# Attention scores in three fp32r products of split q and k, in row halves of TensorE, two units at a time

## The chip, the core and the metric

The kernel runs on one core of one Trainium2 chip. The metric is the time of one execution in device microseconds (us); each value is the median of several runs. One execution was recorded by the hardware profiler, and its page and its trace are what is read below. TensorE is written PE, its weight loads PEld, VectorE DVE, ScalarE ACT, GpSimd POOL, and SyncE, which issues most transfers, SP.

## The reference

An attention with a sigmoid in place of the softmax feeds a mixture of experts that sends each token to one of eight experts:

```python
B, H, S, D = 8, 12, 448, 64
scores = q @ k.transpose(0, 1, 3, 2) / sqrt(D) - log(S)      # per batch and head, 448 x 448
attn = 1 / (1 + exp(-scores))
x = (attn @ v)                                                # to 3584 tokens x 768

logits = x @ w_gate                      # 3584 x 8
e_idx = argmax(logits, axis=1)
gate_w = softmax(logits)[n, e_idx]
for e in range(8):
    h = maximum(x[mask_e] @ w1[e], 0)    # 768 -> 1024
    out[mask_e] = gate_w * sigmoid(x @ w_output_gate)[mask_e, e] * (h @ w2[e])
```

All inputs and the output are fp32. The choice of the expert hangs on the largest of eight logits, so the attention is computed to fp32 accuracy.

## The kernel before

Two heads that share the 128 rows of a tile form a pair (head 0 in rows 0 to 63, head 1 in rows 64 to 127); there are 48 pairs. Two pairs form a group, and the 24 groups run one after the other, each in 7 units (`U = 7`): units 0 to 2 take 128 keys each of the first pair, units 4 to 6 those of the second, and unit 3 the last 64 keys of both pairs. Unit `u` is unit `i` of group `g` (`divmod(u, U)`), 168 units in all.

The loop of `attention` (L698 to L718) goes through the units. In each step it calls `scores(u)` and then `values(u - 2)` (`LAG = 2`). Below, S stands for the scores of one unit and V for the values of one unit.

- `scores` (L619) issues four matmuls of 64 rows by 64 columns of weights, one in each quarter of PE's array (the list `corners`): row half `j` is the head, column half `h` one half of the keys. The operands are fp32, 448 columns stream, and the trace records each such matmul as two instructions, each with its own weight load. The results lie in two banks of PSUM, one for each head; `self.ps_s` has two such pairs of banks, taken in turn. ACT then applies the sigmoid to 128x896 numbers and writes the buffer `at[u % 3]` (L627).
- `values` (L629) issues four matmuls in the same quarters, with 64x64 weights of v and the sigmoids as streaming operand. They add up in four banks (`self.ps_o`). When a pair is complete, DVE copies one bank to `xh` (L637 or L641), adds the other (L647) and transposes into the row buffer (L648).
- After three groups a batch is complete, and `gates` (L671) multiplies its result with the router's weights: 24 matmuls of 64x32 weights and 224 columns, 48 instructions in the trace (L679), at unit 3 of the next group. DVE then forms the routing lists with small operations, and POOL scatters them.
- SP loads q and k two groups ahead (L609, L610) and v (L615, L617), each in three buffers. The loads of a group are issued at unit 0 (q, k) and unit 1 (v).

During the last 50 units (`unit`, L723) the first expert slot is prepared by all engines beside the attention. Then come the expert slots, where PE works on fp32r products of 128x128 weights: each operand is split into a rounded high part and the remainder, and three of the four products are taken (L458 to L460 and L485 to L487).

`carve` gives names to parts of two large buffers, `rounded` (fp32r) and `plain` (fp32), which the expert slots use later. The order on each engine is the order in which the code issues; waits between engines are set by the data.

Of the kernel before, what the change touches and what calls it, by code (L numbers as in the profile page):

```python
# [8 lines left out]
F32 = mybir.dt.float32  # L9
# [3 lines left out]
AF = mybir.ActivationFunctionType  # L13
ALU = mybir.AluOpType
# [5 lines left out]
B, H, S, D = 8, 12, 448, 64  # L20
# [9 lines left out]
G = 2  # L30
# [3 lines left out]
W = 6  # L34
# [7 lines left out]
LATE_N = LATE_MAX + 1  # L42
KT = 8
LG = 3
OOB = 1 << 20
LROWS = E * CAP // 128
ROUNDED = (12 * DF + 12 * TB) * 4
# [4 lines left out]
def r32(ap):  # L52
    return ap.bitcast(F32)


class Kernel:
# [52 lines left out]
    def lists(self, n, g, i):  # L109
        o = i * LG * GB_ * W  # L110
        return self.hb[0:32, o:o + n * g * W].bitcast(I32).rearrange("p (a b w) -> p a b w", b=g, w=W)
# [70 lines left out]
    def init_list(self):  # L182
# [3 lines left out]
        for w in range(1, 4):  # L186
            nc.gpsimd.memset(li[:, :, w:w + 1], w)
        nc.gpsimd.memset(li[:, :, 4:5], OOB)
        nc.gpsimd.dma_start(self.lst.rearrange("(p r) w -> p r w", p=128), li)
# [392 lines left out]
    def attention(self, pool):  # L582
        nc = self.nc
        N = B * NPAIR
        NG = N // G
        GB = NPAIR // G
        U = 7
        t = lambda n, shape: pool.tile(shape, F32, name=n)
        qr = [t(f"q{i}", [128, G, S]) for i in range(3)]
        kr = [t(f"k{i}", [128, G, S]) for i in range(3)]  # L590
        vv = [t(f"v{i}", [128, G, 4, 2, D]) for i in range(3)]
        at = [t(f"a{i}", [128, 2, S]) for i in range(3)]
# [9 lines left out]
        half = [slice(0, 64), slice(64, 128)]  # L602
        corners = [(0, 0), (1, 0), (0, 1), (1, 1)]

        def load_qk(g):
            b, hp = divmod(G * g, NPAIR)
            for r in ([slice(0, G)] if g else [slice(i, i + 1) for i in range(G)]):
                src = lambda a: a[b, hp + r.start:hp + r.stop].rearrange("g p s -> p g s")
                nc.sync.dma_start(kr[g % 3][:, r], src(self.kT))  # L609
                nc.sync.dma_start(qr[g % 3][:, r], src(self.qT))  # L610

        def load_v(g):
            b, hp = divmod(G * g, NPAIR)
            v = vv[g % 3]
            nc.sync.dma_start(v[:, :, 0:3], self.vm[b, hp:hp + G].rearrange("g p c j d -> p g c j d"))  # L615
            for i in range(G):
                nc.sync.dma_start(v[half[i], i, 3], self.ve[b, hp + i])  # L617

        def scores(u):  # L619
            g, i = divmod(u, U)  # L620
            q, k = qr[g % 3], kr[g % 3]
            ps = self.take("s", self.ps_s)
            for j, h in corners:
                e, o = (h, 384) if i == 3 else (i // 4, 128 * (i % 4) + 64 * h)
                qk = nc.tensor.matmul(ps[half[h], j, 0:S], k[half[j], e, o:o + 64], q[half[j], e], start=True, stop=True)  # L625
            self.beat[1] = qk.ins
            self.beat[0] = nc.scalar.activation(at[u % 3], ps[:, :, 0:S], AF.Sigmoid, bias=self.bias_s, scale=1.0 / math.sqrt(D)).ins  # L627

        def values(u):  # L629
            g, i = divmod(u, U)  # L630
            v, a = vv[g % 3], at[u % 3]
            for h, j in corners:
                e, c = (h, 3) if i == 3 else (i // 4, i % 4)
                nc.tensor.matmul(self.ps_o[e][h][half[j], 0:S], v[half[h], e, c, j], a[half[h], j],  # L634
                                 start=(i in ((0, 3 if h else 4)[e],)), stop=(i == (2 + (h == 0), 6)[e]))
            if i == 2:
                nc.vector.tensor_copy(xh, self.ps_o[0][1][:, 0:S])  # L637
            elif i == 3:
                evict(G * g)
            elif i == 6:  # L640
                nc.vector.tensor_copy(xh, self.ps_o[1][1][:, 0:S])  # L641
                evict(G * g + 1)

        def evict(m):
            b, hp = divmod(m, NPAIR)
            x, o = xts[m % NPAIR], xt[b % 2]
            nc.vector.tensor_tensor(x, xh, self.ps_o[m % 2][0][:, 0:S], ALU.add)  # L647
            nc.vector.transpose(o[:, :, 32 * hp:32 * hp + 32], x.rearrange("p (u t) -> p u t", t=32))  # L648
            if hp == NPAIR - 1:
                dst = self.x_dram[b * S:(b + 1) * S].rearrange("(u t) (i x) -> i t u x", t=32, i=4)  # L650
                for i in range(4):
                    e = nc.scalar if m == N - 1 and i % 2 else nc.sync
                    e.dma_start(dst[i], o[32 * i:32 * i + 32])
# [3 lines left out]
        def routing(at, u):  # L657
            if routes and want[0] == at:
                want[0] = next(routes[0])
                if want[0] == "rows":  # L660
                    first = u + 2 if len(rows) != B - 3 else U * NG - 18
                    rows.append((first, routes.pop(0)))
                    if routes:
                        want[0] = next(routes[0])

        def scatters(u):
            for first, r in rows:
                if u - first in (0, 2, 3, 5):
                    next(r)

        def gates(b):  # L671
            gp, gl = self.ps_o[1], self.R["num"].rearrange("p c x -> p (c x)")
            for m in range(NPAIR // 2):
                for p in range(2):
                    e = NPAIR // 2 * p + m
                    for i in range(2):
                        c, tk = slice(64 * p + 32 * i, 64 * p + 32 * i + 32), slice(HS * i, HS * i + HS)
                        for h in range(2):
                            nc.tensor.matmul(gp[h][c, 0:HS], wg[half[h], e], xts[e][half[h], tk], start=(m == 0),  # L679
                                             stop=(m == NPAIR // 2 - 1), tile_position=(64 * h, 64 * p + 32 * i))  # L680
            nc.vector.tensor_copy(gl, gp[1][half[0], 0:HS])
            for h, p in ((1, 1), (0, 0), (0, 1)):
                nc.vector.tensor_tensor(gl, gl, gp[h][half[p], 0:HS], ALU.add)
            routes.append(self.route(b))
            if len(routes) == 1:
                want[0] = next(routes[0])
# [10 lines left out]
        LAG = 2  # L697
        for u in range(U * NG + LAG):  # L698
            g, i = divmod(u, U)
            if i == 0 and 0 < g < NG - 2:  # L700
                load_qk(g + 2)
            self.unit(u - U * NG)
            for r, name in ((2, "counts"), (3, "places")):
                if i == r:
                    routing(name, u)
            if u < U * NG:
                scores(u)
            if u >= LAG:
                values(u - LAG)
            if i == 3 and g and g % GB == 0:  # L710
                gates(g // GB - 1)
            if i == 1 and 0 < g < NG - 2:
                load_v(g + 2)
            if i == 6:
                routing("logits", u)
            scatters(u)
            if u == 10:
                self.init_list()  # L718
# [42 lines left out]
    def build(self, phases="abc"):  # L761
# [17 lines left out]
        def lists():  # L779
            i = 0  # L780
            for tab, lt, lx, n, o in ((self.tab_l, self.lts, self.lxs, LATE_N, EARLY), (self.tab_b, self.ltb, self.lxb, E, 0)):
                for a in range(0, n, LG):
                    b = min(a + LG, n)
                    lq = self.lists(b - a, lx.shape[2], i % 2)
# [86 lines left out]
```

## Time and profile before

| | before |
|---|---|
| median of 3 runs | 770.58 us (769.16 to 772.1) |
| profiled execution | 769.2 us, of which the span from first to last instruction is 767.2 us |
| granted clock of PE | 0.999 of full speed |
| PE busy | 756.8 us (99%) |
| PEld busy | 582.1 us (76%) |
| DVE busy | 398.7 us (52%) |
| ACT busy | 373.4 us (49%) |
| POOL busy | 269.2 us (35%) |

The busy time of an engine is the time in which at least one of its instructions runs. The attention takes the first 269 us of the span, the experts the rest. Matmuls overlap, so a matmul's own duration says less than the distance from its start to the start of the next; the views in order of time give starts. Weight loads run beside matmuls, so their share is no share of the time.

### The profile page before, as it was taken

What the parts mean: (1) busy time and instruction counts of PE and PEld (TensorE: products, weight loads), DVE (VectorE), ACT (ScalarE), POOL (GpSimd) and SP (SyncE); (2) the same over time, 40 slices, a digit from 0 to 9 for tenths busy, and PEclk for the clock granted to TensorE, in tenths of its full rate; (3) what the DMA queues carried; (4) which work ended last, traced back from release to release, by engine and by line L of the source; (5) the groups of instructions that cost most, each with busy time, mean ns of one, the idle gap of its engine ahead of it and who ended that gap; (6) DMA issues with size and microseconds to landing.
All of it is one profiled execution on the core that took longest, in us unless ns stands there. A gap on an engine that the chain in (4) does not pass through costs nothing. (4 is left out here: it accounts for less than half of the span.)

```text
span 767.2 us, 14868 instructions
## 1 busy us (share of the span) xinstructions
PE 756.8 (99%) x5819; PEld 582.1 (76%) x5819; DVE 398.7 (52%) x731; ACT 373.4 (49%) x429; POOL 269.2 (35%) x379
## 2 busy tenths in 40 slices
PE   9999999999999999999999999999999999999996
PEld 4444444444444489999999999999999999999996
DVE  1364746556687769523714525525615524445564
ACT  5666666666787733422523523424424424334544
POOL 5002112020444346258336137127127217316261
PEclk9999999999999999999999999999999999999999
DMA  8475766756796545447446346335345354364531
GB/s 291 132 200 135 204 146 169 205 134 169 262 306 189 156 109 201 141 102 228 125 144 217 113 139 215 120 131 190 110 167 161 130 163 132 130 211 165 176 135 41
DMA packets 73560, 126.53 MB, mean 165 GB/s; under 512 B 15410, under 2 KB 53324, under 8 KB 73472
## 3 DMA queue, kind: packets, MB, share of 16 engines
q1 hardware_dynamic: 62768, 100.18, 43.2%
q0 software_dynamic: 9776, 24.53, 9.5%
q8 instruction: 50, 0.82, 0.5%
q10 hardware_dynamic: 928, 0.69, 0.4%
q14 instruction: 38, 0.31, 0.1%
HBM read 108.77 MB, written 23.09 MB: 172 GB/s over the span
## 5 line engine op out<-in xcount | busy, mean ns | idle before, releaser
L627 ACT ACTIVATE a<-ps,bias_s 128x896 f32<-128x896 f32 x168 | 169.0, 1007 | 86.0 <-PE ps L625 85.4
L384 POOL DMA_INDIRECT plain<-x_dram,lxs x112 | 138.0, 1232 | 73.2 <-ACT h L470 24.7
L625 PE MATMUL ps<-q,k 64*64 64x448 f32 x1344 | 158.1, 542 | 0.0
L634 PE MATMUL ps<-a,v 64*64 64x448 f32 x1344 | 156.2, 536 | 0.2 <-DMA v<-vm 0.2
L458 PE MATMUL ps<-rounded 128*128 128x448 f32 (+1 forms) x432 | 150.7, 349 | 1.2 <-ACTq L822 1.2
L459 PE MATMUL ps<-rounded 128*128 128x448 f32 (+1 forms) x432 | 149.9, 347 | 0.0
L460 PE MATMUL ps<-rounded 128*128 128x448 f32 (+1 forms) x432 | 149.9, 347 | 0.0
L485 PE MATMUL ps<-w2h,h 128*128 128x384 f32 x400 | 133.7, 334 | 0.8 <-DVE y L532 0.8
L487 PE MATMUL ps<-w2h,h 128*128 128x384 f32 x400 | 133.7, 334 | 0.0
L486 PE MATMUL ps<-w2l,h 128*128 128x384 f32 x400 | 133.6, 334 | 0.0
L410 DVE TENSOR_TENSOR rounded<-plain,rounded 128x2048 fp32r<-128x2048 f32 (+5 forms) x63 | 96.9, 1574 | 61.8 <-ACT rounded L409 61.8
L471 DVE SCALAR_TENSOR_TENSOR h<-ps,h 128x384 fp32r<-128x384 f32 (+2 forms) x128 | 45.2, 389 | 155.8 <-ACT h L470 155.7
L470 ACT ACTIVATE h<-ps 128x448 fp32r<-128x448 f32 (+1 forms) x72 | 36.6, 508 | 155.7 <-PE ps L460 152.6
L634 PEld LDWEIGHTS ps<-a,v 64*64 64x64 f32 x1344 | 51.3, 133 | 75.4 <-issue 72.4
L625 PEld LDWEIGHTS ps<-q,k 64*64 64x64 f32 x1344 | 50.8, 134 | 75.3 <-issue 70.6
L458 PEld LDWEIGHTS ps<-rounded 128*128 128x128 f32 x432 | 81.5, 189 | 7.1 <-ACTq L822 1.5
L460 PEld LDWEIGHTS ps<-rounded 128*128 128x128 f32 x432 | 81.5, 189 | 5.0
L459 PEld LDWEIGHTS ps<-rounded 128*128 128x128 f32 x432 | 81.5, 189 | 4.9
L409 ACT CAST rounded<-plain 128x2048 fp32r<-128x2048 f32 (+5 forms) x63 | 81.2, 1332 | 3.8 <-DVE plain L428 3.2
L485 PEld LDWEIGHTS ps<-w2h,h 128*128 128x128 f32 x400 | 75.1, 188 | 1.3 <-DVE y L532 1.1
L514 POOL DMA_INDIRECT out<-y,lts x21 | 26.7, 1269 | 140.6 <-ACT y L491 87.8
L486 PEld LDWEIGHTS ps<-w2l,h 128*128 128x128 f32 x400 | 75.1, 188 | 0.1
(146 smaller groups left out, 689.2 us busy)
## 6 DMA issues: line engine op xcount, KB each, us to landing
plain<-w SPq DMA_DIRECT2D x40, 768.0 KB
plain<-w SPq DMA_DIRECT2D x27, 1024.0 KB
k<-kT SPq DMA_DIRECT2D x23, 448.0 KB
q<-qT SPq DMA_DIRECT2D x23, 448.0 KB
x_dram<-xt SPq DMA_DIRECT2D x30, 336.0 KB
v<-vm SPq DMA_DIRECT2D x24, 384.0 KB
plain<-w SPq DMA_DIRECT2D x6, 512.0 KB
plain<-x_dram,lxs POOLq DMA_INDIRECT x112, 4.1
```

The lines of the kernel that those rows point to most:

```text
L384: self.paced(self.nc.gpsimd.indirect_dma_start(out=self.xg[:, g], out_offset=None, in_=x4, in_offset=bass.IndirectOffsetOnAxis(ap=s["lx"][ ...
L409: self.nc.scalar.copy(hi, raw)
L410: self.nc.vector.tensor_tensor(lo, raw, r32(hi), ALU.subtract)
L458: nc.tensor.matmul(ps, wh[d][:, c], xh[:, d, 0:n], start=(d == 0), stop=False)
L459: nc.tensor.matmul(ps, wh[d][:, c], xl[:, d, 0:n], start=False, stop=False)
L460: mm = nc.tensor.matmul(ps, wl[d][:, c], xh[:, d, 0:n], start=False, stop=(d == 5))
L485: nc.tensor.matmul(ps, hh[:, f, tk], wh, start=(f == 0), stop=False)
L486: nc.tensor.matmul(ps, hh[:, f, tk], wl, start=False, stop=False)
L487: nc.tensor.matmul(ps, hl[:, f, tk], wh, start=False, stop=(f == 7))
L625: qk = nc.tensor.matmul(ps[half[h], j, 0:S], k[half[j], e, o:o + 64], q[half[j], e], start=True, stop=True)
L627: self.beat[0] = nc.scalar.activation(at[u % 3], ps[:, :, 0:S], AF.Sigmoid, bias=self.bias_s, scale=1.0 / math.sqrt(D)).ins
L634: nc.tensor.matmul(self.ps_o[e][h][half[j], 0:S], v[half[h], e, c, j], a[half[h], j], start=(i in ((0, 3 if h else 4)[e],)), stop=(i == (2 ...
```

## The change

For groups 1 to 15, q and k are split into a high part rounded to fp32r and a remainder: `qh`, `ql`, `kh`, `kl`. They lie in the buffer `rounded`, in two sets that groups take in turn. The splits of group g+1 are issued during group g: POOL casts k and q after unit 0, DVE subtracts for `kl` after unit 1 and for `ql` after unit 4.

The scores of these groups, but for unit 3, are three products, `kh*qh + kh*ql + kl*qh`, added up in PSUM. Each is two matmuls of 64 rows by 128 columns of weights, one for each row half (head), in fp32r. Unit 3, whose 64 keys come from two pairs, stays as it was, and so do the values.

For units 8 to 111 the loop takes two units together: the scores of u and u+1, then the values of u-2 and u-1. This needs a fourth buffer for the sigmoids, which lies in `plain`. The load of v moves from unit 1 to unit 2. Scale, sigmoid, gates and experts are untouched.

```diff
+SPLIT_G = range(1, 16)
+TWOS = range(8, 112)
...
+        parts = [[self.carve(4 * G * S * (4 * i + j), G, S) for j in range(4)] for i in range(2)]
+        at.append(self.carve(4 * LROWS * W, 2, S, dt=F32))
+        a_of = lambda u: at[u % 4 if u < TWOS.stop else (u - TWOS.stop) % 3]
+
+        def split_qk(g, i):
+            if g not in SPLIT_G:
+                return
+            qh, ql, kh, kl = parts[g % 2]
+            if i == 0:
+                nc.gpsimd.tensor_copy(kh, kr[g % 3])
+                nc.gpsimd.tensor_copy(qh, qr[g % 3])
+            elif i == 1:
+                nc.vector.tensor_tensor(kl, kr[g % 3], r32(kh), ALU.subtract)
+            elif i == 4:
+                nc.vector.tensor_tensor(ql, qr[g % 3], r32(qh), ALU.subtract)
+
         def scores(u):
...
+            if g in SPLIT_G and i != 3:
+                qh, ql, kh, kl = parts[g % 2]
+                e, o = i // 4, 128 * (i % 4)
+                for t, (k, q) in enumerate(((kh, qh), (kh, ql), (kl, qh))):
+                    for j in range(2):
+                        qk = nc.tensor.matmul(ps[:, j, 0:S], k[half[j], e, o:o + 128], q[half[j], e],
+                                              start=(t == 0), stop=(t == 2))
+            else:
+                for j, h in corners:
...
-            if u < U * NG:
-                scores(u)
-            if u >= LAG:
-                values(u - LAG)
+            if u in TWOS:
+                for t in (u, u + 1):
+                    values(t - LAG - 1) if u % 2 else scores(t)
+            else:
+                if u < U * NG:
+                    scores(u)
+                if u >= LAG:
+                    values(u - LAG)
+            split_qk(g + 1, i)
             if i == 3 and g and g % GB == 0:
                 gates(g // GB - 1)
-            if i == 1 and 0 < g < NG - 2:
+            if i == 2 and 0 < g < NG - 2:
                 load_v(g + 2)
```

On PE, in groups 2 and 3 (units 16 to 25), the program before alternates one S (L625) and one V (L634); x4 is one unit:

```order
L625 MATMUL ps<-q_158,k_161 64x448 x4
L634 MATMUL ps<-a_166,v_163 64x448 x4
L625 MATMUL ps<-q_158,k_161 64x448 x4
L634 MATMUL ps<-a_167,v_164 64x448 x4
L625 MATMUL ps<-q_158,k_161 64x448 x4
L634 MATMUL ps<-a_165,v_164 64x448 x4
```

The same stretch of the changed program, on PE, up to the gates of the first batch (L705). L646 is the new line of the three products, x6 for one unit and x12 for two; L651 is the old form, which unit 3 keeps; L660 is V:

```order
L646 MATMUL ps<-rounded 128x448 x12
L660 MATMUL ps<-a_167,v_164 64x448 x4
L660 MATMUL ps<-plain,v_164 64x448 x4
L646 MATMUL ps<-rounded 128x448 x12
L660 MATMUL ps<-a_165,v_164 64x448 x4
L660 MATMUL ps<-a_166,v_162 64x448 x4
L651 MATMUL ps<-q_156,k_159 64x448 x4
L646 MATMUL ps<-rounded 128x448 x6
L705 MATMUL ps<-x_168,wg 32x224 x4
```

Two units of S stand together and then two of V; the form of the matmuls changes once into L646 and once out of it for each two units, and the gates come between an L646 and a V.

On DVE, in group 3, before, there are only the copies out of PSUM with their additions and transposes (L641, L637, L647, L648):

```order
L637 COPY xh<-ps 128x448
L647 TENSOR_TENSOR x_172<-xh,ps 128x448
L648 STREAM_TRANSPOSE xt_175<-x_172 128x14x32
L641 COPY xh<-ps 128x448
L647 TENSOR_TENSOR x_173<-xh,ps 128x448
L648 STREAM_TRANSPOSE xt_175<-x_173 128x14x32
L681 COPY num<-ps 64x224
```

The same stretch of DVE in the changed program, where L633 makes `kl` and L635 makes `ql`, each from what POOL has cast:

```order
L633 TENSOR_TENSOR rounded<-k_159,rounded 128x896
L635 TENSOR_TENSOR rounded<-q_156,rounded 128x896
L663 COPY xh<-ps 128x448
L673 TENSOR_TENSOR x_172<-xh,ps 128x448
L674 STREAM_TRANSPOSE xt_175<-x_172 128x14x32
L633 TENSOR_TENSOR rounded<-k_160,rounded 128x896
L667 COPY xh<-ps 128x448
L673 TENSOR_TENSOR x_173<-xh,ps 128x448
L674 STREAM_TRANSPOSE xt_175<-x_173 128x14x32
L707 COPY num<-ps 64x224
```

Two subtractions of 128x896 a group have come in ahead of copies that PE's banks wait for.

## Rows read from the trace of the kernel before

**Rows 1.** Page, part 1: busy us (share of the span) xinstructions of each engine.
```profile
PE 756.8 (99%) x5819; PEld 582.1 (76%) x5819; DVE 398.7 (52%) x731; ACT 373.4 (49%) x429; POOL 269.2 (35%) x379
```

**Rows 2.** Windows: stretch and length, busy us of each engine (instructions), clock, DMA.
```profile
15.00:182.00 167.00, 167.00 (x1948) 68.66 (x1944) 89.09 (x217) 108.76 (x119) 19.38 (x36) 1.00 0.62 171
300.00:767.00 467.00, 458.20 (x2589) 443.39 (x2587) 218.44 (x275) 182.93 (x215) 188.90 (x215) 1.00 0.46 149
180.00:200.00 20.00, 20.00 (x220) 8.14 (x216) 14.12 (x50) 14.46 (x18) 4.82 (x9) 1.00 0.74 246
```

**Rows 3.** PE in order of time, plain units: start us, us, line, form, count.
```profile
184.94 0.93 PE L625 MATMUL ps<-q,k 64*64 64x448 f32 x8
185.69 0.93 PE L634 MATMUL ps<-a,v 64*64 64x448 f32 x8
...
189.45 0.93 PE L625 MATMUL ps<-q,k 64*64 64x448 f32 x8
```

**Rows 4.** PE in order of time around the first gates.
```profile
41.60 0.93 PE L634 MATMUL ps<-a,v 64*64 64x448 f32 x8
42.46 1.36 PE L679 MATMUL ps<-x,wg 64*32 64x224 f32 x48
43.76 0.98 PE L625 MATMUL ps<-q,k 64*64 64x448 f32 x8
44.56 0.93 PE L634 MATMUL ps<-a,v 64*64 64x448 f32 x8
```

**Rows 5.** PE in order of time, end of the attention, first fp32r products, last gates.
```profile
267.53 1.68 PE L634 MATMUL ps<-a,v 64*64 64x448 f32 x16
269.14 0.47 PE L458 MATMUL ps<-rounded 128*128 128x448 f32 x1
269.45 0.36 PE L459 MATMUL ps<-rounded 128*128 128x448 f32 x1
...
272.69 0.37 PE L460 MATMUL ps<-rounded 128*128 128x448 f32 x1
272.98 1.37 PE L679 MATMUL ps<-x,wg 64*32 64x224 f32 x48
```

**Rows 6.** PEld in order of time: around the gates, then in fp32r products of 256 columns.
```profile
41.60 0.15 PEld L634 LDWEIGHTS ps<-a,v 64*64 64x64 f32 x4 [0.22 <-issue]
42.46 0.94 PEld L679 LDWEIGHTS ps<-x,wg 64*32 64x32 f32 x48 [0.70 <-issue]
...
693.88 0.19 PEld L458 LDWEIGHTS ps<-rounded 128*128 128x128 f32 x1
694.00 0.19 PEld L459 LDWEIGHTS ps<-rounded 128*128 128x128 f32 x1
```

**Rows 7.** Groups by line and form: busy us, mean ns of one, idle before and releaser.
```profile
L627 ACT ACTIVATE a<-ps,bias_s 128x896 f32<-128x896 f32 x168 | 169.0, 1007 | 86.0 <-PE ps L625 85.4
L410 DVE TENSOR_TENSOR rounded<-plain,rounded 128x896 fp32r<-128x896 f32 x21 | 22.7, 1083 | 0.0
L647 DVE TENSOR_TENSOR x<-xh,ps 128x448 f32<-128x448 f32 x48 | 29.8, 620 | 12.5 <-PE ps L634 10.9
L641 DVE COPY xh<-ps 128x448 f32<-128x448 f32 x24 | 14.9, 622 | 42.2 <-PE ps L634 42.2
```

**Rows 8.** The same view for POOL: operations whose time hangs on columns.
```profile
L187 POOL MEMSET plain<- 128x256 int32 x3 | 1.5, 593 | 0.1
L185 POOL MEMSET plain<- 128x1536 int32 x1 | 1.4, 1415 | 0.0
```

More of the change, by code (lines that the diff above doesn't have):

```diff
@@ L622, in scores @@
             ps = self.take("s", self.ps_s)
-            for j, h in corners:
-                e, o = (h, 384) if i == 3 else (i // 4, 128 * (i % 4) + 64 * h)
-                qk = nc.tensor.matmul(ps[half[h], j, 0:S], k[half[j], e, o:o + 64], q[half[j], e], start=True, stop=True)
+            if g in SPLIT_G and i != 3:
[7 more added lines that the diff above has]
+                for j, h in corners:
+                    e, o = (h, 384) if i == 3 else (i // 4, 128 * (i % 4) + 64 * h)
+                    qk = nc.tensor.matmul(ps[half[h], j, 0:S], k[half[j], e, o:o + 64], q[half[j], e], start=True, stop=True)
             self.beat[1] = qk.ins
-            self.beat[0] = nc.scalar.activation(at[u % 3], ps[:, :, 0:S], AF.Sigmoid, bias=self.bias_s, scale=1.0 / math.sqrt(D)).ins
+            self.beat[0] = nc.scalar.activation(a_of(u), ps[:, :, 0:S], AF.Sigmoid, bias=self.bias_s, scale=1.0 / math.sqrt(D)).ins
         def values(u):
             g, i = divmod(u, U)
-            v, a = vv[g % 3], at[u % 3]
+            v, a = vv[g % 3], a_of(u)
             for h, j in corners:
```

## The prediction, written before the changed kernel was run

> **What bounds the kernel now.** I read the page's busy times first. PE is busy 99% of the span and no other engine above 52% [rows 1], so the question is what PE's work costs, not which engine is late. The windows by stage come next: from 15 to 182 us, the stretch that the change touches, PE is busy in all 167.00 us, while DVE has 89.09, ACT 108.76 and POOL 19.38, at a granted clock of 1.00, which is the 2.4 GHz level [rows 2]. After it, the experts keep PE busy for 458.20 of 467.00 us [rows 2], so a microsecond won or lost in the attention arrives at the end one for one. The groups confirm it from ACT's side: its 168 sigmoids take 1007 ns each and nearly all its idle time ends with PE's scores [rows 7].
>
> Then the view in order of time, since matmuls overlap and only starts count. From 184.94 to 189.45 us lie six units, S and V in turn: 4.51 / 6 = 0.752 us for one unit of either kind [rows 3]. A unit is 4 passes of 448 columns side by side in four quarters, so one pass takes 0.752 / 4 = 0.188 us. With 336 units this is 252.5 of the attention's 269 us; gates and the start are the rest.
>
> **What three products cost.** In row halves one product is one pass of both halves, if the halves run beside each other. Its distance to the next is bounded by two rows. Below: 0.188 us, the pass of a fp32 unit, which has 64-row tiles as here. Above: fp32r products of 448 columns on the whole array, from 269.45 to 272.69 us, 16 of them, 3.24 / 16 = 0.2025 us [rows 5]. The operand type is that of the second row, the tile that of the first; neither is nearer, so I take the middle, 0.195, and keep both. Three products are 0.564 to 0.608 us where S took 0.752: a gain of 0.144 to 0.188 us in each of the 15 x 6 = 90 units changed, 13.0 to 16.9 us by itself.
>
> **What changing the form costs.** The trace has a few places where the matmul's tile changes, and each leaves a gap.
> - Into the gates: the V at 41.60 has streamed by 41.60 + 0.752 = 42.35; the gates' first weight load and matmul start at 42.46, so 0.11 us pass [rows 4, 6]. The time from 272.69 + 0.188 = 272.88 to the gates at 272.98 is again 0.10 [rows 5].
> - After the gap the first weights load with nothing beside them. The first fp32r product starts at 269.14 and the second at 269.45: 0.31, which is 0.108 more than 0.2025, for 128 columns of weights [rows 5]. After the gates the first S takes 43.76 to 44.56, 0.80, which is 0.048 more than 0.752, for 64 columns [rows 4].
>
> So into the row halves costs 0.108 + 0.108 = 0.216 us, and back to the quarters 0.102 + 0.048 = 0.150 us. None of it shows today between S and V, which have one form.
>
> In units 8 to 111 there are 52 double steps, in 15 of which one of the two S is unit 3 and keeps the old form; unit 7 alone makes a sixteenth of that kind. For p the distance of products:
> - 37 with two changed S: before 2 x 0.752 = 1.503. After: 0.216 in, five p, a last pass of 0.188, 0.150 out, that is 0.554 + 5p = 1.494 (p = 0.188) to 1.566 (p = 0.2025). The difference is -0.010 to +0.063 us, times 37: -0.4 to +2.3 us.
> - 16 with one: before 0.752, after 0.554 + 2p = 0.930 to 0.959; +0.178 to +0.207, times 16: +2.9 to +3.3 us.
> - Five gates lie in the stretch (after units 24, 45, 66, 87, 108). Before, each has a change in and a change out; now one of them replaces a change that was counted above. At some 0.15 us each: -0.75 us.
>
> Sum: +1.7 to +4.9 us, with p in the middle +3.3. Two units together halve the number of changes, and with that the gain is just about eaten.
>
> The Trainium skill's page TensorEngine Tiling (Array Packing), section Key Properties, says that changing the tiling mode, not just the tile, drains TensorE; it lists 64x128 and 64x64 as two modes. No row shows this very change, only those between 64x64, 64x32 and 128x128. Without that rule one could hope that row halves and quarters, both of 64 rows, follow each other freely; that is the second rival below.
>
> **What lies beside PE.** DVE gets 30 subtractions of 128x896. The same shape with the same types takes 1083 ns [rows 7], 32.5 us in all, two a group. Over 167 us DVE goes from 53% to about 73%; in its fullest stretch, 180 to 200 us, it is busy 14.12 of 20 us [rows 2], and four more subtractions there would still fit. POOL gets 30 casts of 128x896, which the trace doesn't show. Bounds from POOL's memsets: 1415 ns for 1536 columns, 0.92 ns each, so 0.83 us; 593 ns for 256 spaced columns, 2.3 ns each, so 2.1 us [rows 8]. By either, two casts fit many times into a group of some 10.5 us, so I cost them at nothing; I take 2.1, the dearer one. The subtraction for `kl` waits for POOL's cast, and behind it on DVE stand the copies that free V's banks. A bank is written again about three units later, over 4 us, and copy and addition take 0.62 us each [rows 7], so 1.08 us more in front of them isn't felt by PE. Splits are issued one group ahead, so the scores don't wait for them. If that cover were gone, each late group would cost what it is late, 15 times.
>
> ACT has two sigmoids, some 2.0 us, in a double step of 3.0. The first of them runs during the second S and the first V, so its bank is free before the next S; the fourth sigmoid buffer takes the place that the longer lag needs. q and k have one more reader, but the last reader of their buffers is now unit 3 or the split rather than unit 6, so the loads on SP may start no later than before. The load of v, one unit later, still has more than a group's time. The clock stays where it is, as PE has no long idle stretch. All these I take at zero.
>
> The profiled execution is 769.2 us, 2.0 more than its span, and becomes 772.5. The median of the runs is 1.4 above it, at 770.58; the same +3.3 gives 773.9, and that is the forecast.
>
> **Rivals.**
> 1. *The gap is as shown, but weights are already there.* If the load of the next form's weights goes on during the drain, 0.108 + 0.048 = 0.156 us fall away at 53 double changes: -8.3, so +3.3 becomes -5.0: 765.6. For it: inside a form the next weights load while a matmul runs (64x64 loads start with the V at 41.60; 128-column loads of 0.19 us follow each other every 0.12 us, beside products) [rows 6]. Against it: at every change of form in the trace load and matmul start together after the gap.
> 2. *No gap between row halves and quarters.* Both are of 64 rows. Then only the gain stays, -13.0 to -16.9: some 755. Against it: gates and quarters also have 64 rows each and differ in columns alone, and there the gap is seen [rows 4].
> 3. *The halves run one after the other.* Each of the 270 products then costs a second pass of 0.188: +51, some 825. For it: a fp32r product gives PSUM a result at every column, in two banks at once, and no row has that with one pass; against it: quarters and gates do run two row halves side by side, in two banks.
> 4. *Weights are not loaded ahead within a run of products.* The page TensorE: Matmul & The Clock Gate, section The mechanism, says that weight loads overlap matmuls in flight only where the row group differs. In this kernel each product but the first of a run would then show its load: (37 x 5 + 16 x 2) = 217 times 0.108, +23 on top of +3.3, some 797. The 0.12 us distance with loads of 0.19 us on the same rows [rows 6] speaks against it.
> 5. *The split is late.* A `kl` that waits for POOL holds DVE, then the banks, then PE. It decides from the point where a group's DVE work exceeds its 10.5 us; at 0.5 us for each of 15 groups it is +7.5, some 781. The busy shares above speak against it.
>
> That the change doesn't reach PE is excluded by the new order of its rows.
>
> **How the numbers follow.** Forecast (gaps as in the rows, halves side by side): 0.59, from 772.3 to 775.5. Rival 1: 0.17. Rival 2: 0.09. Rival 3: 0.04. Rival 4: 0.04. Rival 5: 0.07. About 0.5%, 3.9 us, is what a measurement of this kernel can tell from no change, so the line to slower is at 774.4. Of the forecast's 0.59, 0.36 lies below it and 0.23 above. Faster: most of rivals 1 and 2, 0.25. Same: 0.36, and 0.04 from the edges of rivals 1 and 5, 0.40. Slower: 0.23, and 0.12 from rivals 3 to 5, 0.35. The range goes from 761 (rival 1 with p at its lower end and the larger part of the gap gone) to 780; rivals 2, 3 and 4, and a bad rival 5, are left out.
>
> **What the profile after would show.** PE's starts tell nearly all. In a double step: the first L646 some 0.11 us after the last V has streamed, the second product 0.30 us after it, then 0.19 to 0.20 us between products, the two halves starting within a few ns; the whole double step 3.0 to 3.07 us where it was 3.01. Weight loads that start before the last V has ended would show rival 1 or 2; halves 0.19 apart rival 3; products 0.30 apart throughout rival 4; idle PE with DVE or POOL named as releaser rival 5. My forecast is wrong if the double step is shorter than 2.95 or longer than 3.15 us, or if the attention doesn't end 1.7 to 4.9 us later.

## The result and the profile after

The changed kernel takes 782.36 us (781.99 to 783.73, 4 runs), the kernel before 771.34 us (769.16 to 773.19, 4 runs): a ratio of 1.0146, with a 95% interval from 1.0123 to 1.0169. It is slower by 11.0 us, where +3.3 was forecast and the range ended at 780. The span of its profiled execution is 780.7 us, 13.5 longer than before.

Part 1 of the page of the changed kernel, to be held against [rows 1]:

```profile
PE 764.0 (98%) x5639; PEld 597.7 (77%) x5639; DVE 431.4 (55%) x761; ACT 368.2 (47%) x429; POOL 306.0 (39%) x409
```

PE has 180 matmuls fewer (90 units with six in place of eight) and is busy 7.2 us longer. Its share of the span is a little lower: some of the loss is idle time.

PE in order of time in the changed kernel, scores of units 10 to 13 (start us, us, line, form, count). It answers to [rows 3], where a unit of either kind took 0.752 us:

```profile
20.00 0.93 PE L651 MATMUL ps<-q,k 64*64 64x448 f32 x8
20.87 0.87 PE L646 MATMUL ps<-rounded 64*128 64x448 f32 x6
21.67 1.74 PE L660 MATMUL ps<-a,v 64*64 64x448 f32 x16
23.33 1.49 PE L646 MATMUL ps<-rounded 64*128 64x448 f32 x12
24.75 0.98 PE L660 MATMUL ps<-a,v 64*64 64x448 f32 x8
25.55 0.93 PE L660 MATMUL ps<-plain,v 64*64 64x448 f32 x8
```

L651 is unit 3 in the old form, L646 the three products, L660 the values. The old S streams from 20.00 to 20.75, and the row halves start at 20.87: the gap of 0.11 us of [rows 4, 5]. One changed S holds PE from 20.87 to 21.67, two from 23.33 to 24.75: 0.80 and 1.42 us. Their difference is three products, 0.62 us, some 0.205 each. The starts give it more closely: in e1 below, which has no waits, the second product starts 0.311 us after the first (mean of 53 runs of products) and the later ones 0.203 apart (164 distances). So p, the distance of products, is 0.203, and the first weights cost 0.108. Then the first V takes 24.75 to 25.55, 0.80 in place of 0.752.

The next fences show a place where PE is idle. PE in order of time, scores of units 76 and 77:

```profile
127.70 1.74 PE L660 MATMUL ps<-a,v 64*64 64x448 f32 x16
129.37 1.08 PE L646 MATMUL ps<-rounded 64*128 64x448 f32 x8
132.28 0.68 PE L646 MATMUL ps<-rounded 64*128 64x448 f32 x4 [1.83 <-DVE rounded L635]
132.89 0.98 PE L660 MATMUL ps<-a,v 64*64 64x448 f32 x8
```

And DVE in the same stretch, where L633 makes `kl`, L635 makes `ql`, and L230 to L249 are the small operations of the routing lists:

```profile
125.08 1.05 DVE L633 TENSOR_TENSOR rounded<-k,rounded 128x896 fp32r<-128x896 f32 x1
126.04 0.39 DVE L230 STREAM_TRANSPOSE turn<-oh 64x224 f32<-64x224 f32 x1
...
131.02 0.20 DVE L249 TENSOR_REDUCE eom<-sg 64x7 f32<-64x56 f32 x1
131.15 1.07 DVE L635 TENSOR_TENSOR rounded<-q,rounded 128x896 fp32r<-128x896 f32 x1
```

The routing lists hold DVE for 5.1 us, from 126.04 to 131.2, `ql` stands behind them, and its subtraction ends at 132.2. Unit 76, from 129.37, is the last of group 10; of unit 77, the first of group 11, `kh*qh` has streamed, and the second product needs the new `ql`. The same happens once before, at the start of group 5: its first product starts at 59.69 us and its second at 61.88, after 1.82 us of waiting. These are the two places in the attention where PE's idle time is put down to L635; each run of six products there takes 3.51 or 3.52 us instead of 1.42, 2.1 us more. Groups 8 and 14, with lists ahead of their `ql` too, escape by 0.1 us: `ql` ends at 96.96 and 167.34, and the second products start at 97.04 and 167.43.

The attention (up to the first product of the experts) ends here:

```profile
278.93 0.47 PE L460 MATMUL ps<-rounded 128*128 128x448 f32 x1
```

That is 9.8 us later than 269.14 of [rows 5]. The rest is in the experts. PE in order of time at the branch to the slots whose number hangs on the data, in the changed kernel:

```profile
704.43 0.36 PE L460 MATMUL ps<-rounded 128*128 128x256 f32 x1 [3.65 <-ACT y L507]
```

and in the kernel before:

```profile
692.14 0.36 PE L458 MATMUL ps<-rounded 128*128 128x256 f32 x1 [1.19 <-ACTq L822]
```

One wait there is 2.5 us longer, though nothing in the experts' code was changed. What follows it is longer too. Windows from the branch to the end, with the same 480 matmuls, and then of 3.30 us just behind the branch (length, busy us of each engine (instructions), granted clock, DMA), in the changed kernel:

```profile
704.43:780.66 76.23, 69.60 (x480) 69.28 (x480) 41.62 (x46) 35.69 (x44) 30.38 (x25) 0.96 0.38 129
705.60:708.90 3.30, 3.30 (x18) 3.30 (x17) 0.42 (x1) 0.38 (x1) 1.43 (x2) 0.50 0.42 149
```

and in the kernel before:

```profile
692.14:767.16 75.02, 68.06 (x480) 67.74 (x480) 41.54 (x46) 36.27 (x45) 31.49 (x25) 0.99 0.39 131
693.31:696.61 3.30, 3.30 (x30) 3.30 (x29) 0.42 (x1) 0.80 (x2) 1.96 (x2) 1.00 0.24 94
```

Behind its wait of 3.65 us the changed kernel has a granted clock of 0.50, the 1.2 GHz level, and 18 matmuls fall into these 3.30 us, where the kernel before, after 1.19 us, has 30 at 1.00. The time to the end is 1.2 us longer.

### The profile page after: what moved, and what is told of

Its sections match the earlier page's. It is cut to its first block, busy times and chain, and to the rows that moved or that the text cites. A ratio compares the mean times of both kernels' runs of the same rounds, so it can differ in the third digit from the quotient of the medians.

```text
span 780.7 us, 14650 instructions
## 1 busy us (share of the span) xinstructions
PE 764.0 (98%) x5639; PEld 597.7 (77%) x5639; DVE 431.4 (55%) x761; ACT 368.2 (47%) x429; POOL 306.0 (39%) x409
## 5 line engine op out<-in xcount | busy, mean ns | idle before, releaser
L653 ACT ACTIVATE a<-ps,bias_s 128x896 f32<-128x896 f32 x140 | 138.3, 1006 | 97.7 <-PE ps L646 61.5
L660 PE MATMUL ps<-a,v 64*64 64x448 f32 x1120 | 127.8, 545 | 0.2 <-DMA v<-vm 0.2
L660 PEld LDWEIGHTS ps<-a,v 64*64 64x64 f32 x1120 | 38.2, 132 | 56.8 <-issue 52.9
L646 PEld LDWEIGHTS ps<-rounded 64*128 64x128 f32 x540 | 46.4, 184 | 43.8 <-ACT plain L653 11.3
L487 PEld LDWEIGHTS ps<-w2h,h 128*128 128x128 f32 x400 | 75.1, 188 | 1.3 <-DVE y L534 1.2
L489 PEld LDWEIGHTS ps<-w2h,h 128*128 128x128 f32 x400 | 75.1, 188 | 0.0
```

The costliest lines, as they stand in the source:

```text
L487: nc.tensor.matmul(ps, hh[:, f, tk], wh, start=(f == 0), stop=False)
L489: nc.tensor.matmul(ps, hl[:, f, tk], wh, start=False, stop=(f == 7))
L646: qk = nc.tensor.matmul(ps[:, j, 0:S], k[half[j], e, o:o + 128], q[half[j], e], start=(t == 0), stop=(t == 2))
L653: self.beat[0] = nc.scalar.activation(a_of(u), ps[:, :, 0:S], AF.Sigmoid, bias=self.bias_s, scale=1.0 / math.sqrt(D)).ins
```

## The experiments

Theory A says that the time is TensorE's: changes of form with their gap and load, as forecast, but with p at its upper end, and two waits for `ql`. The rivals are B, that the split's work on DVE and POOL slows the attention in many places, and C, that taking units in twos costs. Each is compared with runs of the kernel before on the same chip.

### e1: ql earlier

```diff
             elif i == 1:
                 nc.vector.tensor_tensor(kl, kr[g % 3], r32(kh), ALU.subtract)
-            elif i == 4:
                 nc.vector.tensor_tensor(ql, qr[g % 3], r32(qh), ALU.subtract)
```

> The subtraction for ql is issued after unit 1, together with the one for kl, so it stands ahead of the small routing operations on DVE; all else is the changed kernel. Theory A (the time is TensorE's own, form changes with their gaps and weight loads, plus two stalls of 1.9 us where ql came late): both stalls vanish, 3.9 us less than the changed kernel, some 778.5 us, and the double steps stay at 3.08 and 3.22 us. Theory B (DVE's and POOL's extra work slows the attention in many places): no more than 1 us is won, 781 to 783. Theory C (the grouping in twos is what costs): 782, unchanged.

Measured: 778.14 us (before 770.31; ratio 1.0104, 1.0081 to 1.0128). That is 4.2 us less than the changed kernel (3.2 less when each is held against its own runs of the kernel before, +7.8 and +11.0), where A said 3.9; B and C expected 1 us or nothing. The trace decides more closely than the medians: neither wait is left, and the attention is 4.8 us shorter. PE in order of time at the units that had waited:

```profile
125.10 1.74 PE L659 MATMUL ps<-a,v 64*64 64x448 f32 x16
126.76 1.49 PE L645 MATMUL ps<-rounded 64*128 64x448 f32 x12
128.18 0.98 PE L659 MATMUL ps<-a,v 64*64 64x448 f32 x8
```

The two S take 1.42 us again, with no idle time. On DVE `ql` now stands ahead of the lists:

```profile
122.47 1.05 DVE L633 TENSOR_TENSOR rounded<-k,rounded 128x896 fp32r<-128x896 f32 x1
123.44 1.08 DVE L634 TENSOR_TENSOR rounded<-q,rounded 128x896 fp32r<-128x896 f32 x1
124.44 0.40 DVE L230 STREAM_TRANSPOSE turn<-oh 64x224 f32<-64x224 f32 x1
```

The lists start at 124.44, and the attention ends at 274.15, 5.0 us after that of the kernel before.

### e2: twos only

```diff
-            split_qk(g + 1, i)
...
-            if g in SPLIT_G and i != 3:
-                ... three products in row halves
+            (all units: one fp32 product in quarters, as before)
```

> The kernel before with two units' scores and then two units' values in units 8 to 111, with the fourth sigmoid buffer and the later load of v; no split, scores in fp32 quarters as before. Theory A: within 1 us of the kernel before, 770 to 772, with a double step of 3.01 us. Theory C: slower by 5 us or more, as the longer lag or the two score banks make TensorE wait.

Measured: 770.75 us (before 770.31; ratio 1.0001, 0.998 to 1.0022). In its trace a double step runs from 65.48 to 68.49, 3.01 us, and the attention ends at 268.27. C falls: the order in twos, with its fourth buffer, costs nothing that can be seen.

### e3: row halves in fp32, without the split

```diff
             if g in SPLIT_G and i != 3:
-                ... three fp32r products
+                e, o = i // 4, 128 * (i % 4)
+                for j in range(2):
+                    qk = nc.tensor.matmul(ps[:, j, 0:S], k[half[j], e, o:o + 128], q[half[j], e], start=True, stop=True)
...
-            split_qk(g + 1, i)
```

> As the kernel with twos only, but the scores of groups 1 to 15 without unit 3 are one fp32 product in 64x128 row halves: the form changes as in the changed kernel, there is no split and no work for DVE and POOL, and the passes are four as before. Theory A: each of 53 double changes of form costs 0.366 us, the gates save 0.75: +18.6 us over the kernel before, some 790 us; double steps of 3.37 us. Theory B: no split, so no slowdown: 771. A rival to A, that the gap belongs to fp32r and not to the form of the tile: 771 as well.

Measured: 788.34 us (before 770.31; ratio 1.024, 1.0213 to 1.0266), +18.0; the attention, ending at 287.19, is 18.1 us longer. PE in order of time, where L644 is the row halves, L648 the old form and L657 the values:

```profile
65.41 1.77 PE L644 MATMUL ps<-q,k 64*128 64x448 f32 x8
67.11 0.98 PE L657 MATMUL ps<-a,v 64*64 64x448 f32 x8
67.91 0.93 PE L657 MATMUL ps<-plain,v 64*64 64x448 f32 x8
68.66 0.93 PE L648 MATMUL ps<-q,k 64*64 64x448 f32 x8
69.53 1.02 PE L644 MATMUL ps<-q,k 64*128 64x448 f32 x4
70.48 1.74 PE L657 MATMUL ps<-a,v 64*64 64x448 f32 x16
```

Against e2 only the tile differs, with the same four passes, the same type and no split: one S now holds PE 0.95 us, from 69.53 to 70.48, where it was 0.752, with a gap of 0.11 before it. The change of form alone costs what the prediction had for it (18.6 by its terms). B is out as the cause of the most part, and so is a gap that belongs to fp32r.

### e5: three products in the quarters

The form of the values, 64x64, is kept for the products too, so that it never changes. The type is fp16, since the fp32r form that the changed kernel uses has results in all 128 rows.

```diff
-TWOS = range(8, 112)
+TWOS = range(0, 0)
...
+        F16 = mybir.dt.float16
+        ... parts are fp16 tiles in the buffer plain
...
+            if g in SPLIT_G:
+                qh, ql, kh, kl = parts[g % 2]
+                for t, (k, q) in enumerate(((kh, qh), (kh, ql), (kl, qh))):
+                    for j, h in corners:
+                        e, o = (h, 384) if i == 3 else (i // 4, 128 * (i % 4) + 64 * h)
+                        qk = nc.tensor.matmul(ps[half[h], j, 0:S], k[half[j], e, o:o + 64], q[half[j], e],
+                                              start=(t == 0), stop=(t == 2))
```

> Three products of split q and k in 64x64 quarters, the form that the values have, so that the form never changes; the parts are fp16 in place of fp32r; one unit of scores and one of values in turn as in the kernel before; unit 3 is split too, 105 units in all; POOL casts and DVE subtracts as in the changed kernel, ql early. Theory A: each unit wins 0.752 - 3p, with p from 0.188 to 0.2025 us: -15.1 to -19.7 us, 751 to 756 us. Theory B (the split work on DVE and POOL is what costs): the same split work costs here too, so 765 or more.

Measured: 752.46 us (before 770.31; ratio 0.9771, 0.9745 to 0.9796), faster than both kernels. PE in order of time, L648 the three products, L662 the values:

```profile
63.75 0.75 PE L648 MATMUL ps<-plain 64*64 64x448 f16 x12
64.32 0.93 PE L662 MATMUL ps<-a,v 64*64 64x448 f32 x8
65.07 0.75 PE L648 MATMUL ps<-plain 64*64 64x448 f16 x12
```

S takes 0.57 us, three products of 0.19, and V follows at its usual 0.75: no gap. The casts and subtractions are the same in number and size as in the changed kernel, so their work isn't what costs there. It isn't quite free here, though: 105 units at 0.185 us should win 19.4 us, and the attention, ending at 253.01, is 16.1 shorter. In four groups with routing lists, PE waits 0.6 us for an addition on DVE (L675) that stands behind both subtractions and the lists, 2.4 us in all, the first of them here:

```profile
57.67 0.98 PE L662 MATMUL ps<-a,v 64*64 64x448 f32 x8 [0.60 <-DVE x L675]
```

Neither the kernel before nor e7 has such a wait. The parts of fp16 are rounded otherwise than those of fp32r; how accurate the scores are with them for other inputs isn't shown here.

### e6: row halves, one unit at a time

```diff
-TWOS = range(8, 112)
+TWOS = range(0, 0)
```
(on top of e1)

> The changed kernel with ql early, but one unit of scores and one of values in turn, so the form changes into the row halves and back for each of the 90 changed units. Theory A: each unit costs 0.554 + 2p - 0.752 = +0.209 us with p = 0.2034, 18.8 us in all, less 0.75 at the gates: some 18 over the kernel before, 788 to 790 us, 10 to 11 more than with two units together. Theory B (the split's work on DVE and POOL): as with two units together, 778.

Measured: 791.64 us (before 771.8; ratio 1.0257, 1.0228 to 1.0285), above the 788 to 790 expected. PE in order of time, L645 the products, L659 the values:

```profile
63.50 0.87 PE L645 MATMUL ps<-rounded 64*128 64x448 f32 x6
64.30 0.98 PE L659 MATMUL ps<-a,v 64*64 64x448 f32 x8
65.21 0.87 PE L645 MATMUL ps<-rounded 64*128 64x448 f32 x6
```

Each S and V together take 1.71 us, where they were 1.503, and the attention ends at 287.00, 17.9 us later than before, which is the 18 that A said. The rest lies in the experts, whose wait at the branch is 4.1 us here. With 90 changes of form in place of 53 the loss of the attention goes from 5.0 to 17.9 us.

### e7: the split alone

```diff
-            if g in SPLIT_G and i != 3:
-                ... three products in row halves
+            (all units: one fp32 product in quarters, in turn with the values)
```
(on top of e6; what POOL and DVE make is read by nothing)

> The casts on POOL and the subtractions on DVE for groups 1 to 15 are done (ql early), but nothing reads them: scores in fp32 quarters, one unit of scores and one of values in turn as in the kernel before. Theory A: DVE's and POOL's work lies beside TensorE's, 770 to 772. Theory B: some 2 us or more over the kernel before, which would be the part of the remaining 7.8 us that the forms don't explain.

Measured: 770.47 us (before 771.8; ratio 0.9991, 0.997 to 1.0011); the attention ends at 268.96. In the changed kernel, B has nothing left but the two late `ql`.

### e8: row halves in fp16

```diff
+        F16 = mybir.dt.float16
+        ... parts are fp16 tiles in the buffer plain
```
(on top of e1)

> The changed kernel with ql early and parts of fp16 in place of fp32r: the same 64x128 row halves, the same order in twos. It tells what makes a product 0.203 us in the row halves and 0.189 in fp16 quarters. If the type does (theory A1): p falls to 0.189, (37 x 5 + 16 x 2) x 0.0145 = 3.1 us less than in fp32r, 775. If the row halves of 128 columns do (theory A2): p stays at 0.203 and the time at 778. Either way the gaps at the changes of form stay, and the first product's extra time of 0.11 us too if it is the load of 128 columns; half of it if it goes by bytes.

Measured: 769.65 us (before 771.8; ratio 0.9972, 0.9957 to 0.9987), lower than either expectation. PE in order of time, L648 the three products, L662 the values:

```profile
62.84 0.74 PE L648 MATMUL ps<-plain 64*128 64x448 f16 x6
63.51 1.74 PE L662 MATMUL ps<-a,v 64*64 64x448 f32 x16
65.18 1.31 PE L648 MATMUL ps<-plain 64*128 64x448 f16 x12
66.42 0.98 PE L662 MATMUL ps<-a,v 64*64 64x448 f32 x8
```

One S holds PE 0.67 us, two 1.24: three products are 0.57, p is 0.19. So the type makes the 0.203, not the row halves. And 0.67 less two products, 0.188 and 0.102 leaves nothing for the first weights, where fp32r had 0.108; by starts, the second product follows the first after 0.200 us, 0.01 more than p. The groups by form from 15 to 180 us show the loads; first those of e8:

```profile
L648 PEld LDWEIGHTS <-plain 64*128 64x128 f16 x536 | 21.9, 94 | 51.0 <-issue 33.2 <-POOL plain L633 1.4 <-POOL meta L252 1.4
```

then those of the changed kernel:

```profile
L646 PEld LDWEIGHTS ps<-rounded 64*128 64x128 f32 x516 | 44.3, 184 | 42.3 <-ACT plain L653 11.3 <-ACT a L653 10.6 <-issue 8.5
```

A load of the same 64x128 weights takes 94 ns in fp16 and 184 in fp32r. The attention of e8 ends at 265.40, 8.75 us before that of e1; 217 products after the first of a run by 0.014 and 53 loads by 0.10 make 8.3. The Trainium skill's page TensorE: Matmul & The Clock Gate, section Weight-path perf modes, has a fast weight load for 128 weights of types other than FP32; the two rows agree with it. Half the bytes alone don't explain them: in e5, whose 64 columns are not the 128 that the page asks for, a load in fp16 takes 107 ns, longer than that of 128 columns here:

```profile
L648 PEld LDWEIGHTS <-plain 64*64 64x64 f16 x1260 | 37.9, 107 | 57.0 <-issue 49.1 <-POOL meta L252 0.9
```

The fp32 loads of 64 columns in e5 take 133 ns, so half the bytes save 26 ns there and 90 ns with 128 columns.

### e9 and e10: the wait in the experts

The wait at the branch is 3.7 us in the changed kernel, e1 and e8 and 4.1 in e6, and 0.9 to 1.3 in the kernel before, e2, e3, e5 and e7. The first four share the number of PE's matmuls, 5639, 180 fewer than before; e3 with 5459 and e5 with 6239 have the short wait, so it isn't a matter of fewer or more. ACT, which the row of the changed kernel names, isn't what PE waits for: in e1 its operation ends at 698.63 and PE starts at 699.70. Both kernels here (e9 is e1, e10 the kernel before) get:

```diff
+        for _ in range(180):
+            nc.tensor.matmul(self.ps_o[1][0][:, 0:8], warm[:, 0:128], warm[:, 0:8], start=True, stop=True)
         LAG = 2
```

> The kernel with ql early, with 180 more matmuls of 8 columns at the start, so that TensorE has as many instructions as in the kernel before. It is about one wait of TensorE in the experts, at the branch to the slots whose number hangs on the data: 3.7 to 4.1 us in the kernels with three products in row halves, 0.9 to 1.3 us in all others. Theory P (the wait hangs on where the code behind the branch lies in TensorE's instruction stream): it falls to 0.9 to 1.3 us. Theory R (it comes from the time at which the branch is reached, or is chance): it stays at 3.7, or takes other values. The start grows by some 5 to 15 us, so the whole time isn't compared.

> The kernel before with the same 180 matmuls of 8 columns at the start, as a control. Theory P: the code behind the branch is shifted by 180 matmuls with their loads, in the other direction than in the changed kernel, so the wait may take either value. Theory R, if the time of arrival decides: it changes too, as the branch is reached 5 to 15 us later. If it stays at 1.2 while the other kernel's wait stays at 3.7, neither theory holds.

Measured, one run each: 813.33 and 810.81 us, the start being some 39 us longer, where 5 to 15 were expected. PE at the branch in e9:

```profile
736.58 0.39 PE L460 MATMUL ps<-rounded 128*128 128x256 f32 x1 [1.62 <-ACTq L854]
```

With the count of before the wait falls from 3.7 to 1.6 us, a little above the 1.3 that theory P allowed; in e10 it stays at 1.1. That speaks for the place of the code in PE's stream and against something that the row halves do to the experts. But the padding also moves the branch by some 38 us, which left the wait of the kernel before as it was and may not have left that of e1. It is likely, not shown.

## Why the prediction was wrong, step by step

1. *What bounds the kernel*: right. What PE loses arrives at the end, and other engines' added work doesn't (e7), but for point 4. By the signs that the prediction named, the double step, 3.08 us, lies inside its bounds of 2.95 and 3.15, and the end of the attention, 9.8 us later, far outside its 1.7 to 4.9; idle PE with DVE as releaser was its sign for rival 5.
2. *The changes of form*: right, mechanism and size. Gap 0.11, first load 0.108, way back 0.15 were read from [rows 4, 5]; e3 has 18.1 us in the attention where the same terms give 18.6. Rivals 1 and 2 fall with it, and rival 4 with p. Halves run side by side, their starts within 4 ns (e1), so rival 3 falls. The Trainium skill's page TensorEngine Tiling (Array Packing), section Key Properties, has the rule that a change of tiling mode drains TensorE; the gap of 0.11 us between quarters and row halves in e3, and none in e5, where the form stays, agree with it, which no row of before had shown.
3. *The distance of products*: mis-sized. The middle of two rows, 0.195, was taken; it is 0.203, at the upper row, that of fp32r, and e8 shows that the type decides. By 0.203 the terms give 37 x 0.066 + 16 x 0.208 - 0.75 = +5.0 in place of +3.3; e1's attention has +5.0 over that of before and +5.2 over e7's.
4. *"Splits are issued one group ahead, so the scores don't wait for them"*: wrong, and this is the largest miss. It counted the busy share of DVE (73%) and the length of a group, not what stands ahead of `ql` in DVE's queue. In groups with routing, 5.1 us of list operations are issued at units 2 and 3 and `ql` after unit 4, behind them; twice DVE reached it only when the next group's scores had begun. Rival 5 is near in name only: its path went from a `kl` that waits for POOL through DVE's copies to the banks, at 0.5 us in all groups. `kl` did wait for POOL four times, up to 0.7 us, and PE didn't feel it; what PE felt was `ql` itself, 2.1 us in each of two groups. The changed kernel's attention is 4.8 us longer than e1's, 4.2 of it in these two places and 0.4 in the start. Which groups suffer goes with the pairing in twos: the first scores of groups 5 and 11 come second in a double step, 10.1 us after those of the group before, those of groups 8 and 14 come first, after 11.8.
5. *Nothing for the experts, and a clock that stays where it is*: wrong by 2.5 us, the wait at the branch, whose cause is open, and by 1.2 us behind it, where the clock is at the lower level for 3.4 us. e1, e6 and e8 have the lower level around the branch too, the kernel before and e7 don't.

Sum: 5.0 and 4.8 in the attention, 2.5 at the branch and 1.2 behind it are 13.5 us, the difference of the two profiled spans. The medians differ by 11.0. The profiled execution of the kernel before is the fastest of its four, and over all its runs it varies from 768.15 to 773.75 us. Of those with a clock on record, all up to 770.5 have a mean granted clock of 0.997 or more, all above 771.2 one of 0.996 or less. In the traces of e2, e3 and e10 the clock falls to 0.50 around the end of another wait of the experts, 2.2 to 3.0 us long; that this also makes the longer times of the kernel before is likely, but its one trace doesn't show it.

## What to carry to other kernels

A matmul that gets cheaper in another form of tile must pay for the way in and out: here some 0.36 us per visit (e3), while three fp32r products win 0.14 us for each unit, so that even two units together don't pay for the visit. Three products in the neighbours' own form (fp16, 64x64) took 16 us off the attention, and in row halves in fp16, with the first load hidden, 3.7. Where an unknown cost lies between two rows, ask which property the price hangs on (here the type) before taking the middle. And an operation that is hidden by its engine's free time isn't hidden yet: look at what stands ahead of it in that engine's queue in the fullest stretch, since moving `ql` by three units was worth 4 us.

## What else the runs showed of the hardware

POOL's casts of 128x896 took 1026 and 1014 ns (k and q), near the lower of the two bounds from its memsets [rows 8]; in e1 they took 932 and 1021 ns, and into fp16 in e8 932 and 969 ns, which overlaps with them. POOL's small operations L252, 64 rows of one to three numbers, took 191 ns on average before. In the changed kernel, of the 20 in the first 180 us, the eight that run beside a subtraction of DVE took 0.91 to 1.24 us and the twelve others 0.18 to 0.20.

The 180 matmuls of 8 columns in e9 took 38.4 us, 0.213 each, as much as a product of 448 columns. PE in order of time:

```profile
4.17 38.39 PE L723 MATMUL ps<-rounded 128*128 128x8 f32 x180
42.50 4.64 PE L650 MATMUL ps<-q,k 64*64 64x448 f32 x24
46.97 0.92 PE L659 MATMUL ps<-a,v 64*64 64x448 f32 x8
```

The three units of S right behind them still took 1.49 us each, twice the 0.752 of later units, and the 13 matmuls of 256 columns ahead of them took 0.226 each, against 0.120 behind the branch in e9. So PE ran at half its later pace before and behind them, most likely in between too, and 0.213 isn't to be held against products at the full clock.
